# Banded attention and a top-1 mixture of experts: heads in row halves, loads reordered, one jump per expert

## The chip, the cores and the metric

The kernel runs on one core of one Trainium2 chip. The metric is the device time of one execution in microseconds. It was run three times: 770.36, 775.02 and 781.09 us, median 775.02. One further execution was taken with the hardware profiler; all rows of a profile below come from it.

The engines go by short names: PE is the matrix engine, with PEld for its loads of the stationary operand; DVE, ACT and POOL are the vector, scalar and general engine; SP issues most transfers. The transfers of all queues run on 16 DMA engines. PSUM holds PE's products; 512 columns of fp32 on 128 partitions are called a bank.

## What is computed

First a banded attention over 8 batches, 8 heads, 576 positions and 64 dimensions. Four heads look at the last 32 positions, four at every fourth of the last 128. Then the output, as 4608 tokens of 512 numbers, goes through a mixture of 8 experts, one expert a token.

```python
scores = scale * np.matmul(q, k.transpose(0, 1, 3, 2))
mask_plain = (rel >= 0) & (rel < window)                       # window 32
mask_dil = (rel >= 0) & (rel < window * dilation) & (rel % dilation == 0)
attn = softmax(np.where(masks, scores, -1e9))
x = np.matmul(attn, v) -> (4608, 512)
e_idx = np.argmax(x @ w_gate, axis=1)
for e in range(8):                                             # w1: 512 x 1024, w2: 1024 x 512
    h = np.maximum(x[mask] @ w1[e], 0.0)
    out[mask] = gate_w * sigmoid(x @ w_output_gate)[:, e] * (h @ w2[e])
```

## The kernel before

**Attention.** The host reorders the dilated heads by position modulo 4, so that all heads have the same band: a block of 32 queries needs its own block of 32 keys and the one before. The batches go in four pairs, each in nine steps (`NSTEP`); a step `g` holds four query blocks, on four strips of 32 partitions, for all 8 heads. Heads lie in pairs `hp`, two on 128 partitions (64 dimensions each).

Before the change the keys `kb` and the values `vb`, `v2` of a head pair stand as a block diagonal: head `c` fills 64 partitions, the other 64 are zero (`clear`). So one product of 128 rows does both heads:

```python
nc.tensor.matmul(sp[32*a : 32*a+32, P*hp : P*hp+P], lhsT=qb[b % 2][:, hp, 32*i : 32*i+32], rhs=keys, ...)
```

A step has 16 such products for the scores (L313) and 16 for the values (L370), each of 128 columns; in fp32 each shows as two passes in the profile. The step also has the mask, added by a product with the identity (L305), the maximum, subtraction and exponential (L326, L330, L336), the sums of a head on POOL (L341, L345, L347), the transposition of the probabilities (L358, copied by ACT at L360), the division (L384, L392), and the transposition of x for the routing (L426, copied at L432 and L435). The values are kept twice, `vb` and, shifted by 32 positions, `v2`; of `v2` half the lanes are loaded and half are copied from `vb` by DVE and ACT (`shift_v`, L290).

The loads of Q, K and V (`load_qk`, L273 and L276, and `load_v`, L282 and L285) are issued on SP, in between the stores of x to a scratch `xs` in DRAM (L402, L407). There are two sets of buffers, for the two batches of a pair; the loads of the next pair go out as soon as a batch is done. x has four buffers.

**Routing.** For each pair of batches, nine tokens to a partition: products with the gate weights, their transposition, the choice of an expert (`route_pick`), the rank within the expert (`rank_products`, `route_rank`), one-hot placements (`route_pay`, `route_spots`), and products that place the token numbers (`place_idx`, `place_scale`). The steps at which these parts run are written in two tables, `calm` and, for the third pair, `brisk`. Everything in the kernel keeps the order in which it is written (`manual_schedule`).

**Experts.** A token tile has 128 tokens; expert 0 starts with three tiles of the first three pairs (`head`) while the routing of the last pair runs beside it (`during_first`, `during_second`). The other experts take four tiles each (`BASE`), with up to two more where there are more tokens. Weights and activations are split into two parts of lower precision (`split_w`, L128 on ACT and L132 mostly on DVE), and each product is three (L204 for the first matrix, L835 for the second). Rows are gathered by POOL from `xs` (`gather4`, L162, four transfers a tile), turned by DVE and cast by ACT (`prep4`, L184, L191), and the results are scattered by POOL (L848). While an expert runs its second matrix, the weights and rows of the next are prepared; its first block of products (`start`) is issued at the end of the expert before. What depends on the number of tokens is reached by nested tests (`rest`, L1190), from the rarest case to the common one:

```python
with tc.If(flag[e] > bound) as more:
    body()
with more.Else():
    rest(less)
```

## Time and profile before

| | |
|---|---|
| three runs | 770.36, 775.02, 781.09 us |
| span of the profiled execution | 711.3 us |
| mean granted clock of PE | 0.940 |
| busy in the span | PE 597.4, PEld 476.4, DVE 351.5, ACT 261.1, POOL 372.3 us |
| transfers | 96.76 MB, mean 136 GB/s |

The span reaches from the first to the last instruction. The profiled execution's own time is not recorded beside it; the median of the runs is 63.7 us longer than the span, which is what lies around it. A row of grouped instructions names the line, engine, operation, `out<-in` and the count, then the busy time and the mean of one in ns, then the idle time ahead and what ended it. A row of waits names who waited for whom, the total in us, how often, and the longest. A row of a timeline begins with the start and the length in us. A row of a stretch gives its length, the busy time of PE, PEld, DVE, ACT and POOL, the granted clock, the share of the DMA engines, and GB/s.

### The profile page before, as it was taken

Reading aid. Unit: us, or ns where it says so; the run is one execution under the profiler, and the core shown is the slowest. Engines: PE = TensorE matmul, PEld = TensorE weight load, DVE = VectorE, ACT = ScalarE, POOL = GpSimd, SP = SyncE. Lnnn points to the kernel's source line nnn. Section 1 sums busy time; section 2 is a strip of 40 time slices with the busy share of each in tenths; the row PEclk is TensorE's granted clock in tenths of the full one; section 3 lists DMA queues with packets and bytes.
Section 4 is the critical chain, followed back from the end, with each engine's and each line's share of the span. In section 5 each row is a group of like instructions: output and inputs, shape, how many; then the busy total and the mean of one; then the engine's idle time right before and its main releaser. Section 6 shows DMA issues by size and latency. Waiting matters only on the chain. (4 is left out here: it accounts for less than half of the span.)

```text
span 711.3 us, 13438 instructions
## 1 busy us (share of the span) xinstructions
PE 597.4 (84%) x5077; PEld 476.4 (67%) x5109; DVE 351.5 (49%) x620; ACT 261.1 (37%) x449; POOL 372.3 (52%) x497
## 2 busy tenths in 40 slices
PE   5685877877677799998599999499999959989992
PEld 4464655655456789786488788388778748858891
DVE  5453476594796574364175164256237417526020
ACT  4464555545563322343153243143234214324010
POOL 7753446474474376476475177277247647525110
PEclk8998998998899799999799999899999979999997
DMA  8999899889945342154155144244205415511010
GB/s 203 217 257 213 195 237 242 220 198 228 265 109 178 98 146 77 50 158 146 44 162 159 37 141 134 99 135 144 89 23 173 138 47 159 157 45 30 16 46 30
DMA packets 55784, 96.76 MB, mean 136 GB/s; under 512 B 10107, under 2 KB 40317, under 8 KB 55680
## 3 DMA queue, kind: packets, MB, share of 16 engines
q1 hardware_dynamic: 46800, 76.44, 40.8%
q0 software_dynamic: 8880, 18.91, 8.3%
q8 instruction: 68, 1.11, 0.7%
q14 instruction: 36, 0.29, 0.2%
HBM read 79.57 MB, written 19.27 MB: 139 GB/s over the span
## 5 line engine op out<-in xcount | busy, mean ns | idle before, releaser
L162 POOL DMA_INDIRECT sd<-xs,idx x112 | 130.4, 1164 | 34.0 <-issue 31.8
L204 PE MATMUL ph<-sc,w 128*128 128x512 f32 x480 | 115.8, 399 | 20.6 <-issue 17.4
L204 PEld LDWEIGHTS ph<-sc,w 128*128 128x128 f32 x480 | 91.6, 193 | 43.9 <-issue 20.6
L848 POOL DMA_INDIRECT out_dram<-yt,idx x39 | 38.6, 990 | 98.9 <-ACT yt L844 52.7
L162 POOL DMA_INDIRECT xg<-xs,idx x56 | 60.8, 1086 | 47.6 <-PE ph L204 22.6
L341 POOL TENSOR_TENSOR half<-pt 128x256 f32<-128x256 f32 x34 | 26.1, 767 | 67.4 <-ACT pt L336 67.0
L835 PE MATMUL y<-w,h 128*128 128x512 f32 x190 | 53.7, 390 | 0.0
L210 ACT ACTIVATE h<-ph 128x512 fp32r<-128x512 f32 (+1 forms) x48 | 28.1, 586 | 67.1 <-PE ph L204 62.1
L211 DVE SCALAR_TENSOR_TENSOR h<-ph,h 128x512 fp32r<-128x512 f32 (+1 forms) x48 | 32.3, 675 | 37.0 <-ACT h L210 36.9
L345 POOL TENSOR_TENSOR half<-half 128x128 f32<-128x128 f32 (+3 forms) x136 | 43.2, 318 | 10.7
L132 DVE TENSOR_TENSOR w<-wraw,w 128x1024 fp32r<-128x1024 f32 x36 | 44.0, 1227 | 8.1 <-ACT w L128 8.1
L392 DVE TENSOR_TENSOR x<-av,rs 128x512 f32<-128x512 f32 x36 | 24.8, 688 | 45.1 <-DMA xs<-x 23.8
L191 ACT CAST sc<-sd 128x512 fp32r<-128x512 f32 x28 | 17.4, 620 | 75.6 <-DVE sd L184 60.5
L204 PE MATMUL ph<-sc,sa 128*128 128x512 f32 (+1 forms) x132 | 35.8, 408 | 9.3 <-issue 8.2
L835 PE MATMUL z<-w,h 128*128 128x512 f32 x152 | 43.5, 389 | 0.0
L128 ACT CAST w<-wraw 128x1024 fp32r<-128x1024 f32 x40 | 41.6, 1044 | 0.0
L835 PEld LDWEIGHTS y<-w,h 128*128 128x128 f32 x190 | 35.5, 188 | 7.3
L370 PE MATMUL av<-sc,pT 128*32 128x128 f32 x288 | 26.7, 312 | 15.5 <-ACT pT L360 7.2
L426 PE MATMUL tp<-idn,x 128*128 128x128 f32 x144 | 24.3, 293 | 17.3 <-DVE x L392 15.0
L204 PEld LDWEIGHTS ph<-sc,sa 128*128 128x128 f32 x132 | 26.1, 205 | 14.4 <-issue 8.7
L326 DVE TENSOR_REDUCE mx<-sp 128x8 f32<-128x512 f32 x36 | 23.8, 662 | 21.6 <-PE sp L313 21.6
L426 PEld LDWEIGHTS tp<-idn,x 128*128 128x128 f32 x144 | 15.8, 145 | 27.9 <-DVE x L392 14.3
(284 smaller groups left out, 1344.5 us busy)
## 6 DMA issues: line engine op xcount, KB each, us to landing
wraw<-in_w_dram SPq DMA_DIRECT2D x64, 512.0 KB, 4.3
xs<-x SPq DMA_DIRECT2D x40, 128.0 KB, 5.8
vb<-in_vv_dram SPq DMA_DIRECT2D x8, 448.0 KB, 6.4
qb<-in_qT_dram SPq DMA_DIRECT2D x3, 896.0 KB, 9.8
kb<-in_kT_dram SPq DMA_DIRECT2D x6, 448.0 KB, 10.6
sb<-in_vv_dram SPq DMA_DIRECT2D x8, 320.0 KB, 5.0
sd<-in_qT_dram SPq DMA_DIRECT2D x4, 512.0 KB, 7.8
sa<-in_kT_dram SPq DMA_DIRECT2D x8, 256.0 KB, 6.9
```

The costliest lines, as they stand in the source:

```text
L128: nc.scalar.copy(out=W[e, kind][0][c], in_=raws[e, kind, c])
L132: sub.tensor_tensor(out=w[1][c], in0=raws.pop((e, kind, c)), in1=w[0][c], op=ALU.subtract)
L162: nc.gpsimd.indirect_dma_start(out=xg[j][:, P * a : P * a + P], out_offset=None, in_=xs4, in_offset=bass.IndirectOffsetOnAxis(ap=idx4[:, a ...
L204: nc.tensor.matmul(ph[:, 0:m], lhsT=part_of(w, a, o, P), rhs=x[:, c, 0:m], start=k == 0, stop=k == 3 * NC - 1)
L210: nc.scalar.activation(out=hh, in_=ph[:, 0:m], func=AF.Relu)
L211: nc.vector.scalar_tensor_tensor(out=hl, in0=ph[:, 0:m], scalar=0.0, in1=hh, op0=ALU.max, op1=ALU.subtract)
L341: nc.gpsimd.tensor_tensor(out=half, in0=pv[:, :, 0:32], in1=pv[:, :, 32:64], op=ALU.add)
L345: nc.gpsimd.tensor_tensor(out=dst, in0=half[:, :, 0:n], in1=half[:, :, n : 2 * n], op=ALU.add)
L370: nc.tensor.matmul(av[32 * a : 32 * a + 32, P * hp : P * hp + P], lhsT=pT[:, hp, 32 * a : 32 * a + 32], rhs=src[:, :, hp, i // 2, :], star ...
L426: nc.tensor.transpose(out=tp[:, c], in_=x[:, P * c : P * c + P], identity=idn)
L835: nc.tensor.matmul(y, lhsT=l[:, r], rhs=part_of(w, a, DM * fc, DM), start=fc == 0 and n == 0, stop=fc == NF - 1 and n == 2)
L848: put = nc.gpsimd.indirect_dma_start(out=out, out_offset=bass.IndirectOffsetOnAxis(ap=at.bitcast(U32), axis=0), in_=yt, in_offset=None, bo ...
```

## The change

**Attention.** Keys and values stand without zero blocks: head `c` of a pair has its own 64 partitions in all of Q, K and V, which are loaded with 128 partitions. Scores and values become 32 products each of 64 rows and 64 columns (`scores`, `values`): two heads in the two row halves and four query blocks in the four column strips. Their results lie in two PSUM tiles of two banks (`sa`), one bank for each half, scores in the first 256 columns and values in the last. For the first two pairs the shifted V is copied whole by DVE and ACT (`first_shift`), for the last two half of it is loaded as before; for the last pair ACT copies the other half. x lies in halves of the stage buffers until step 26, and is copied for the routing in one piece (the order by classes moves into the read of `gate_products`). The first loads go out in the order of need, K and the first masks on ACT's queue.

**Order in a step.** The exponential moves into the next step; the transposition of x comes four steps behind its scores (three from step 27 on). PE's instructions of one step of the third pair, before, from the transposition of the probabilities to the first products of the values:

```order
L358 MATMUL tp<-idn,pt 128x128 [waits PE_49]
L358 MATMUL tp<-idn,pt 128x128 x3
L305 LDWEIGHTS cb
L305 MATMUL sp<-mk,cb 128x512
L313 MATMUL sp<-kb_108,qb_109 32x128 x16
L426 MATMUL tp<-idn,x 128x128 [waits DVE_49,Activation_49]
L426 MATMUL tp<-idn,x 128x128 x3
L370 MATMUL av<-v_111,pT 32x128 [waits DVE_49,Activation_49]
L370 MATMUL av<-vb_110,pT 32x128 [waits DMAHW3_49,DMAHW1_49]
```

And after, from the scores of one step to the values of the next:

```order
L330 MATMUL s_95<-sa_104,sd_106 32x64 x32
L379 MATMUL tp<-idn,pt 128x128 [waits DVE_49,Activation_49]
L379 MATMUL tp<-idn,pt 128x128 x3
L317 LDWEIGHTS cb
L317 MATMUL s_94<-mk,cb 128x256 [waits DVE_49]
L317 LDWEIGHTS cb
L317 MATMUL s_94<-mk,cb 128x256
L453 MATMUL tp<-idn,wraw 128x128 [waits Activation_49]
L453 MATMUL tp<-idn,wraw 128x128 x3
L393 MATMUL s_95<-sc_110,pT 32x64 [waits DVE_49,Activation_49]
L393 MATMUL s_95<-sb_108,pT 32x64
```

The products on the full array (transpositions, mask) now stand together, and so do those in strips: the scores stand behind the values of an earlier step instead of between the transpositions.

**Routing.** The parts run at other steps, most of them later, and over more steps for the first two pairs. The nine comparisons of `route_spots` become one, the counts are taken along with the ranks. In the first expert the ranks of the last pair come one block of products later, and its four subtractions of weights go from POOL to DVE.

**Experts.** The number of the case is computed on the chip (`path`), read at the middle of an expert (`choose`), together with a hint for the jump, and one `Switch` replaces the nested tests; the check for rare repairs behind expert 0 is such a jump too. PE at the end of the first expert that has the tests, before:

```order
L835 MATMUL z<-sb,h_3436 128x512
L204 MATMUL ph<-sc,w_3414 128x512 [waits Activation_49]
L204 MATMUL ph<-sc,w_3414 128x512 [waits DVE_49]
L204 MATMUL ph<-sc,w_3414 128x512 x10
L1182 TENSOR_LOAD cnt
L1190 COMPARE_AND_BRANCH
L204 MATMUL ph<-sc,w_3414 128x512 x12
L204 MATMUL tpx<-xxh,w_3415 128x256 [waits PE_49]
```

And after:

```order
L881 MATMUL z<-sb,h_4398 128x512
L206 MATMUL ph<-sc,w_4376 128x512 [waits Activation_49]
L206 MATMUL ph<-sc,w_4376 128x512 [waits DVE_49]
L206 MATMUL ph<-sc,w_4376 128x512 x10
L1430 SWITCH_STRIDE
L1430 ISA x2
L1267 BRANCH_PREFETCH_HINT
L206 MATMUL ph<-sc,w_4376 128x512 x12
L1430 UNCONDITIONAL_BRANCH
```

The load of the count has gone to the middle of the expert; behind the jump stands, in each of the five bodies, a hint for its own end. The gathers of rows change their order: of expert `e+1` the tiles 2 and 3 go ahead of the rare tiles of `e`, and tiles 0 and 1 of `e+2` are gathered at the end of `e`. The rare tiles are turned during the second matrix instead of at the end of the first, and every second pair of blocks of the first matrix takes PSUM banks of another pool.

```diff
-        ps_s = actx.enter_context(tc.tile_pool(name="ps_s", bufs=2, space=PSUM))
-        ps_a = actx.enter_context(tc.tile_pool(name="ps_a", bufs=2, space=PSUM))
+        ps_s = actx.enter_context(tc.tile_pool(name="ps_s", bufs=1, space=PSUM))
+        sa = [ps_s.tile([P, 2, 512], F32, name=f"s{i}") for i in range(2)]
...
+        def load_q(b, j0, j1):
+            s = slice(64 * j0, 64 * j1)
+            nc.sync.dma_start(out=qb[b % 2][:, :, s], in_=qT[b, :, :, s])
+
+        def load_k(eng, b, j0, j1):
+            eng.dma_start(out=kb[b % 2][:, j0:j1], in_=kT[b, :, j0:j1])
...
+        def load_vv(b):
+            load_v(b, 0, 9)
             for c in range(2):
+                r = lanes(c, 1)
+                nc.sync.dma_start(out=v2[b % 2][r, :, 1:9], in_=vv[b, r, :, 0:8])
...
+        def mask(g):
+            m = mk[:, subs_of(g)[0]].rearrange("p (h c k) -> p h c k", h=4, c=2)
+            for c in range(2):
+                nc.tensor.matmul(
+                    sa[g % 2][:, c, 0:256].rearrange("p (h k) -> p h k", h=4), lhsT=idb, rhs=m[:, :, c],
+                    start=True, stop=False, skip_group_check=True,
+                )
...
         def scores(g):
-            var, subs = subs_of(g)
-            sp = ps_s.tile([P, 512], F32, name="sp")
-            nc.tensor.matmul(sp, lhsT=idb, rhs=mk[:, var], start=True, stop=False, skip_group_check=True)
+            _, subs = subs_of(g)
             for hp in range(4):
-                for a, (b, i) in enumerate(subs):
-                    je = i // 2
-                    jo = (i - 1) // 2 if i else 0
-                    keys = _free(
-                        kb[b % 2], je * 256 + hp * 32, [[2304, 2], [128 + (jo - je) * 256, 2], [1, 32]]
-                    )
-                    nc.tensor.matmul(
-                        sp[32 * a : 32 * a + 32, P * hp : P * hp + P],
-                        lhsT=qb[b % 2][:, hp, 32 * i : 32 * i + 32],
-                        rhs=keys,
...
-                    )
-            st[g, "s"] = sp
+                for c in range(2):
+                    r = slice(64 * c, 64 * c + 64)
+                    for a, (b, i) in enumerate(subs):
+                        je = i // 2
+                        jo = (i - 1) // 2 if i else 0
+                        nc.tensor.matmul(
+                            sa[g % 2][32 * a : 32 * a + 32, c, 64 * hp : 64 * hp + 64],
+                            lhsT=qb[b % 2][r, hp, 32 * i : 32 * i + 32],
+                            rhs=_free(kb[b % 2][r], je * 256 + hp * 32, [[128 + (jo - je) * 256, 2], [1, 32]]),
...
+                        )
...
         def values(g):
             _, subs = subs_of(g)
             pT = st.pop((g, "p"))
-            av = ps_a.tile([P, DM], F32, name="av")
             for hp in range(4):
-                for a, (b, i) in enumerate(subs):
-                    src = vb[b % 2] if i % 2 else v2[b % 2]
-                    nc.tensor.matmul(
-                        av[32 * a : 32 * a + 32, P * hp : P * hp + P],
-                        lhsT=pT[:, hp, 32 * a : 32 * a + 32],
-                        rhs=src[:, :, hp, i // 2, :],
...
-                    )
-            st[g, "av"] = av
+                for c in range(2):
+                    r = slice(64 * c, 64 * c + 64)
+                    for a, (b, i) in enumerate(subs):
+                        src = vb[b % 2] if i % 2 else v2[b % 2]
+                        o = 256 + 64 * hp
+                        nc.tensor.matmul(
+                            sa[(g + 1) % 2][32 * a : 32 * a + 32, c, o : o + 64],
+                            lhsT=pT[r, hp, 32 * a : 32 * a + 32],
+                            rhs=src[r, hp, i // 2, :],
...
+                        )
...
-            x = wk.tile([P, DM], F32, name="x", bufs=4)
+            if g >= 26:
+                x = wk.tile([P, DM], F32, name="x", bufs=4)
+            else:
+                if g % 2 == 0:
+                    st["rows"] = stage.tile([P, 1024], F32, name="wraw")
+                x = st["rows"][:, DM * (g % 2) : DM * (g % 2) + DM]
...
-                nc.scalar.copy(out=xT[:, 0:2, o + s0 : o + s0 + n], in_=tp[:, 0:2, p0 : p0 + n])
-                for c, i0, q0, m in class_pieces(s0, n):
-                    f0 = o + NCLS * i0 + c
-                    nc.scalar.copy(
-                        out=xT[:, 2:4, f0 : f0 + NCLS * (m - 1) + 1 : NCLS], in_=tp[:, 2:4, p0 + q0 : p0 + q0 + m]
-                    )
...
+                nc.scalar.copy(out=xT[:, :, o : o + n], in_=tp[:, :, p0 : p0 + n])
...
         def route_spots(pr):
             ohp = R["ohp"] = rt.tile([P, NSTEP, P], BF16, name="ohp")
-            for c in range(NSTEP):
-                nc.vector.tensor_scalar(
-                    out=ohp[:, c], in0=iot, scalar1=R["pos"][:, c : c + 1], scalar2=None, op0=ALU.is_equal
-                )
+            TP = [P, NSTEP, P]
+            nc.vector.tensor_tensor(
+                out=ohp, in0=bc(iot.unsqueeze(1), TP), in1=bc(R["pos"].unsqueeze(2), TP), op=ALU.is_equal
+            )
...
-        clear(nc.vector, kb[0], 0)
...
-        clear(nc.vector, vb[1], 0)
+        for t in v2:
+            nc.gpsimd.memset(t[:, :, 0], 0.0)
...
-        nc.sync.dma_start(out=cb, in_=cbf)
-        nc.sync.dma_start(out=mk[:, 0:1], in_=cmask[:, 0:1])
-        load_qk(0, 0, 2)
+        nc.sync.dma_start(out=idb, in_=cbf[:, 0:P])
+        load_q(0, 0, 2)
...
+        nc.scalar.dma_start(out=mk[:, 0:1], in_=cmask[:, 0:1])
+        load_k(nc.scalar, 0, 0, 2)
+        nc.scalar.activation(out=warm, in_=zero, func=AF.Exp)
+        nc.scalar.dma_start(out=mk[:, 1:2], in_=cmask[:, 1:2])
+        load_k(nc.scalar, 0, 2, 4)
+        load_k(nc.scalar, 0, 4, 9)
...
-            4: dict(late=[rank_products], post=[route_rank]),
+            3: dict(late=[rank_products, route_rank]),
...
         for g in range(last + 1):
             if g >= 2:
                 transpose_p(g - 2)
-                inverse(g - 2)
+            if g < last:
+                mask(g)
+            if g >= 1:
+                softmax(g - 1)
+            if 4 <= g <= hurry:
+                transpose_x(g - 4)
+            if g >= hurry:
+                transpose_x(g - 3)
...
             if g >= 2:
                 values(g - 2)
-            routing(g, "ahead")
+                inverse(g - 2)
+                output(g - 2)
+                load(g - 2, load_vv if g > NSTEP + 2 else whole_v)
             if g < last:
-                softmax(g)
-            if g >= 2:
-                output(g - 2)
-                load(g - 2, load_v)
-            if g in (last - 3, last - 1):
-                late_sum(g)
-            shift(0, g)
+                scores(g)
+                shifted(g)
...
             if 33 <= g < 36:
-                split_lo(0, 0, g - 33, nc.gpsimd)
+                split_lo(0, 0, g - 33, nc.vector)
...
+    def choose(e):
+        flag[e] = nc.values_load(cnt[0:1, 2 * E + 3 + e : 2 * E + 4 + e], min_val=0, max_val=len(PATHS))
+        flag[e, "hint"] = tc.switch_hint({t: flag[e] for t in ENGINES}, len(PATHS) + 1, f"paths{e}")
...
-        elif k == 1:
+        elif k == 2:
             rank_products(pr)
             route_rank(pr)
             load_w(1, 0)
-        elif k == 2:
+        elif k == 3:
             route_pay(pr, nc.vector)
             route_rows(pr)
             route_spots(pr)
-        elif k == 4:
+        elif k == 5:
             place_idx(pr)
             finish_idx(perm, pm, idx, E * SLOTS, rt)
-            nc.vector.tensor_copy(out=st[pr, "lt"][1][:, 0 : E * SLOTS], in_=idx)
+            nc.vector.tensor_copy(out=st[pr, "lt"][:, 512 : 512 + E * SLOTS], in_=idx)
             for j in range(HEAD, HEAD + 2):
                 gather(j, where(0, j)[0])
-        elif k == 5:
             scale_exp(pr)
             scale_pick(pr)
             scale_gate(pr)
-        if k < 4:
-            split_w(0, 1, k, nc.gpsimd)
+        if 0 < k < 5:
+            split_w(0, 1, k - 1)
...
+    for n in tc.Switch(flag["rare"], 2, flag["rare", "hint"]):
+        products1(1, 1, *X, BASE * P, ph, (1, 2, 3))
+        if n:
+            repair()
...
-            h.append(base_h(e, fc, X, BASE * P))
+            h.append(base_h(e, fc, X, BASE * P, ph=bank(ps_x, "tpx") if fc % 4 > 1 else None))
             if fc == 2:
-                gather4(e, 4)
-                gather4(e, 5)
-                next_gathers(e + 1)
+                rows_of(e + 1, *((2, 3) if e > 1 else range(BASE)))
+                rows_of(e, 4, 5)
             if fc < 6:
                 split_w(e, 1, fc - 2)
                 if fc == 5 and e + 1 < E:
                     load_w(e + 1, 0)
-            if fc >= 6:
-                prep4(fc - 2, *xx, fc - 6)
+        choose(e)
         ys = [bank(ps_y, "y"), bank(ps_z, "z"), bank(ps_y, "y"), bank(ps_z, "z")]
         for fc in range(NF):
             for j in range(BASE):
@@ -1174,23 +1238,16 @@
                 if fc == 3:
                     load_w(e + 1, 1)
                 prep4(fc, *X, fc)
+            if fc in (4, 5):
+                prep4(fc, *xx, fc - 4)
+            if fc == 5:
+                rows_of(e + 2, 0, 1)
...
-        def rest(paths):
-            (bound, body), *less = paths
-            if not less:
-                body()
-                return
-            with tc.If(flag[e] > bound) as more:
-                body()
-            with more.Else():
-                rest(less)
...
+        bodies = [
+            nothing,
+            lambda: extra(e, BASE, xx, 0, 1, fill),
+            lambda: extra(e, BASE, xx, 1, 0, fill),
+            lambda: extra(e, BASE, xx, 1, 1, fill),
+            two,
+        ]
+        for n in tc.Switch(flag[e], len(bodies), flag[e, "hint"]):
+            bodies[n]()
```

355 lines of the change are left out of this document (186 added, 169 removed).

## The prediction

> **What bounds the kernel now.** I read the slices of the page first, then stretches of my own choosing, then the waits, the transfers, and last the instructions of single steps. In the slices each digit is the busy share of a fortieth of the span (17.8 us).
>
> ```profile
> PE   5685877877677799998599999499999959989992
> DMA  8999899889945342154155144244205415511010
> GB/s 203 217 257 213 195 237 242 220 198 228 265 109 178 98 146 77 50 158 146 44 162 159 37 141 134 99 135 144 89 23 173 138 47 159 157 45 30 16 46 30
> ```
>
> For eleven slices the DMA engines are full at 200 to 260 GB/s while PE is at 5 to 8 tenths; afterwards it is the other way round, with PE at 9 and single dents. The same by stage, with the exponentials (one a step) that set the borders:
>
> ```profile
> L336 ACT ACTIVATE pt<-pt x36: 612/631/664, 9.7 to 203.9; 128x512 f32<-128x512 f32 x36
> 9.70:203.90 194.20, 141.68 (x2681) 106.09 (x2712) 115.06 (x272) 97.35 (x205) 105.19 (x255) 0.90 0.95 224
> 203.90:292.00 88.10, 77.95 (x541) 67.13 (x542) 53.64 (x120) 29.60 (x56) 48.71 (x42) 0.94 0.34 112
> 292.00:697.10 405.10, 371.78 (x1779) 297.99 (x1777) 175.39 (x223) 126.06 (x183) 208.48 (x187) 0.97 0.33 102
> ```
>
> Columns of a stretch: length, busy PE, PEld, DVE, ACT, POOL, granted clock, DMA share, GB/s. The 36 attention steps take 194.2/35 = 5.55 us each; PE is busy 141.7 of 194.2, DVE 115.1, ACT 97.4, POOL 105.2, and only the DMA engines (0.95) are full. Who waits there says the same (first 200 us):
>
> ```profile
> DVE x L392 <- DMA xs<-x: 23.8, 9, 5.6
> ACT sc L290 <- DMA sb<-in_vv_dram: 21.1, 5, 7.6
> ACT v L290 <- DMA vb<-in_vv_dram: 18.4, 6, 5.1
> PE sp L313 <- DMA sa<-in_kT_dram: 6.3, 2, 5.6
> ```
>
> V arrives late at the copies, K late at PE, and the rows of x leave late, so that their four buffers are not free. Attention is bound by transfers. From 292 us on PE is the bound, with 405.1 - 371.8 = 33.3 us idle; between the two lies the first expert with 88.1 - 78.0 = 10.1 us idle.
>
> **The transfers.** Bytes do not explain the 224 GB/s; the shape does. Alone on the engines were part of a Q load on 128 partitions (71.1 to 71.65 us), of a K load on 64 (73 to 76) and of the V loads on 64 and 32 (133.5 to 136.8):
>
> ```profile
> 71.10:71.65 0.55, 0.55 (x20) 0.50 (x13) 0.00 (x0) 0.55 (x1) 0.46 (x2) 0.50 1.05 381
> 73.00:76.00 3.00, 2.86 (x48) 1.72 (x41) 1.08 (x2) 2.11 (x5) 0.04 (x1) 1.00 0.96 186
> 133.50:136.80 3.30, 3.15 (x65) 2.42 (x61) 2.17 (x6) 1.45 (x3) 2.01 (x5) 1.00 1.08 209
> ```
>
> The last number is GB/s: 381 against 186 and 209. The change loads K and V with 128 partitions. Q, K and V are 9.44 MB each (8*576*512*4 bytes). At 381 GB/s the three take 74 us; rows of x, 9.44 MB, at 300 (my choice between 224 and 381, for 1 KB pieces) 31 us; the shifted V that is still loaded (four of eight batches, half the lanes, 2.1 MB) at 209 GB/s 10 us; weights and constants some 8 us. Together 123 us where 194 were full. So transfers stop being the bound if the step is longer than 123/36 = 3.4 us.
>
> **What a step costs then.** In one step of before, undisturbed by transfers, PE shows:
>
> ```profile
> 101.50 1.33 PE L313 MATMUL sp<-sa,sd 128*32 128x128 f32 x32
> 105.05 0.66 PE L358 MATMUL tp<-idn,pt 128*128 128x128 f32 x4
> 105.85 0.81 PEld L313 LDWEIGHTS sp<-sa,sd 128*32 128x32 f32 x32 [0.32 <-issue]
> 105.85 1.08 PE L313 MATMUL sp<-sa,sd 128*32 128x128 f32 x32
> 106.90 0.65 PE L426 MATMUL tp<-idn,x 128*128 128x128 f32 x4
> 248.58 0.55 PE L939 MATMUL tp<-lt,idn 128*32 128x48 f32 x32
> ```
>
> The 16 products of the scores are 32 passes, four column strips side by side, in 1.08 us; the values have the same shape. After the change there are twice as many, of 64 columns and 64 rows, eight side by side. No row of before has 64-row halves, so I bound them. Upper end: the halves do not overlap, and 64 passes of half the columns cost the same 1.08 us. Lower end: they overlap fully, half, 0.54. L939 gives 32 passes of 48 columns, four abreast, in 0.55 us with the tail of the last (0.21); that is 0.34 us of starts, 10.7 ns each, so 64 starts need at most 0.69 us. I take 0.66 a group, nearest to that row: a gain of 0.42, twice a step. The order within a step also changes: both transposes and the mask first, then values and scores, so that PE changes between the full array and strips twice instead of four times; one such change is the 0.32 us of "issue" above. PE's step: 0.66 + 0.65 + 0.2 (mask, estimated) + 2*0.66 + 2*0.32 = 3.5, less what the tails overlap, say 3.3 us.
>
> DVE, ACT and POOL keep nearly all of their work. DVE's share:
>
> ```profile
> L392 DVE TENSOR_TENSOR x<-av,rs 128x512 f32<-128x512 f32 x17 | 11.7, 687 | 26.6 <-DMA xs<-x 16.6 <-PE av L370 10.0
> L330 DVE TENSOR_TENSOR pt<-sp,mx 128x512 f32<-128x512 f32 x16 | 11.1, 692 | 1.5
> L326 DVE TENSOR_REDUCE mx<-sp 128x8 f32<-128x512 f32 x16 | 10.5, 658 | 6.9 <-PE sp L313 6.9
> L384 DVE RECIPROCAL rs<-sm 128x8 f32<-128x8 f32 x16 | 3.0, 188 | 0.0
> L567 DVE TENSOR_SCALAR ohp<-cb,pos x36: 234/244/2439, 117.7 to 239.0; 128x128 bf16<-128x128 bf16 x36
> L132 POOL TENSOR_TENSOR w<-wraw,w x4: 2331/2353/2370, 223.5 to 239.0; 128x1024 fp32r<-128x1024 f32 x4
> L132 DVE TENSOR_TENSOR w<-wraw,w x36: 1214/1225/1268, 255.0 to 612.7; 128x1024 fp32r<-128x1024 f32 x36
> ```
>
> Four a step make 0.69 + 0.69 + 0.66 + 0.19 = 2.2 us, 80 of the 115 busy us. The other 35 are shifts of V and routing. Nine spot comparisons (9*0.244) become one of the same elements, perhaps 1.2 us: minus 3 for three pairs. Three subtractions of weights come from POOL: plus 3*1.225 = 3.7. So DVE stays near 116 us, of which 36, or 1.0 a step, are uneven. If they lie on five steps of nine, those take 2.2 + 0.3 for the hand-overs (estimated) + 1.8 = 4.3 us, and the other four PE's 3.3: (5*4.3 + 4*3.3)/9 = 3.9. Between this and 4.35, the distance from one scores group to the next in the step of before (105.85 - 101.50), I take 4.0, nearer to the first. The routing that moves to a later step keeps its instructions on DVE, POOL and PE, and the first gathers still go out three steps before the end; the same sum holds it. ACT gets one copy a step for x transposed in place of two to five: it has 97 us of work before, less after, and is no bound. The eight half-tile memsets go; POOL's and ACT's are hidden today behind the first transfers, and DVE's too; the first exponential, at 9.7, comes perhaps 1 us sooner since the first K and mask go out on ACT's queue. K on ACT's queue costs ACT five issues at the start, while it has nothing else. Q, K and V of a batch become one transfer each where there were two or three, on SP: fewer issues, no new wait. Rows of x pass to eight half buffers until step 26, so that a late landing holds up nobody.
>
> Steps of 4.0 in place of 5.55: 35*1.55 = 54 us, plus 1 at the start: **55**. Ends: PE's 3.3 (80 us) and the 4.35 (43 us).
>
> **The first expert.** Three waits of PE belong to routing:
>
> ```profile
> PE tp L504 <- DVE oh L495: 4.0, 1, 4.0
> PE perm L573 <- DVE ohp L567: 3.4, 2, 2.1
> ```
>
> One block of products more stands between the choice and the ranks, and the placing comes a block later: the 4.0 goes, the 3.4 goes in part. Against that, DVE takes four subtractions from POOL, 4*1.225 = 4.9 us, in the same stretch; they are late next, ahead of the placing. The load of the second expert's weights goes out a block later too, and is read some eight blocks after that. Between 0 and 7.4 I take **5**.
>
> **The other experts.**
>
> ```profile
> L1190 PEldq COMPARE_BRANCH  x26: 70/340/4714, 334.6 to 692.7; - x26
> 334.09 2.81 PE L204 MATMUL ph<-sc,w 128*128 128x512 f32 x11 [0.22 <-DVE sc L192]
> 346.06 4.31 PE L204 MATMUL ph<-sc,w 128*128 128x512 f32 x11 [9.16 <-issue]
> PE ph L204 <- issue: 25.6, 3, 9.2
> PE ph L204 <- ACT sc L191: 3.2, 3, 1.3
> PE y L1053 <- DMA out_dram<-yt,idx: 1.9, 1, 1.9
> PE y L1043 <- ACT sa L210: 1.6, 1, 1.6
> ```
>
> Where an expert has no more than four tiles, PE walks through nested tests, three of them taken at over 3 us each (the maximum is 4.7), and stands still for 8.2 to 9.2 us; three experts do so, 25.6 us. Afterwards eleven products take 4.31 us instead of 2.81, at the reduced clock: 3*1.5 = 4.5 us more. The change has one jump by an index that was read a half expert earlier, with a hint to fetch the target. What a hinted jump costs no row shows. Lower end 0.07 us (the minimum above, no fetch); upper end 3.5 for the jump and 3.5 for leaving the body. Cover: the queue holds the twelve products of the next expert's first block, 2.8 us, and the body that most take holds twelve more. I take 0.6 for each of seven: 25.6 + 4.5 - 4.2 = 26. The rows of the next expert are gathered two tiles earlier, ahead of the rare tiles; the 3.2 us of waits for the cast go, less what the later rare tiles cost, 2. The gathers are the same in number, POOL is busy 208 of 405 us there, so they stay hidden. Together **28**.
>
> The Trainium skill (Runtime: NRT & Kernel Launch, Instruction fetch mechanics) says prefetch is sequential and a taken jump outside the window must fetch before it goes on; the rows above agree at over 3 us. It knows no hint, and by it alone the jump would still fetch: that is the second rival's result.
>
> **The sum.** The page's span is 711.3 us; the median of three runs is 775.0, so 63.7 us lie around the span (59 to 70 over the runs 770.4 to 781.1), and I keep 63.7. 711.3 - 55 - 5 - 28 = 623; 623 + 64 = **687 us**.
>
> **Rivals.**
> 1. Transfers stay the bound. If 128-partition K and V run at the mean of today, 224 GB/s, then 42 MB take 188 us; attention gains only 6, the time is 775 - 6 - 5 - 28 = 736. For it: the 381 was seen in short stretches. Against: every Q load shows it. Chance 0.08.
> 2. Hints do not help: 7 us of fetch for each of seven, less 2.8 + 1.5 of cover, leaves 2.7*7 = 19 us where I had 4: 687 + 15 = 702. Chance 0.15.
> 3. PE becomes the bound by its starts:
>
> ```profile
> 97.08 0.37 PE L511 MATMUL tp<-oh,ones 128*128 128x8 bf16 x9
> ```
>
> Eight columns wide, nine products still need 0.37 us, (0.37 - 0.17)/8 = 25 ns from start to start. If the 128 passes of a step had that floor, they would take 3.2 us in place of 1.3: the step is 3.3 + 1.9 = 5.2 us, attention gains 13, and the time is 729. L939's 10.7 ns speaks against it, with strips of columns but not of rows. Chance 0.07. The Trainium skill (TensorEngine Tiling (Array Packing), Instruction Overhead) says this: some 60 cycles for each product, and no tiling of a dimension that is already small; by it halving 128 columns to 64 gains nothing. L939 disagrees.
> 4. Slower than before: each change of the 64-row half drains PE as the change of strips does, 0.32 us. The loop changes halves eight times in a group, 16 a step: 5.1 us more, steps of 8.4, attention 35*2.85 = 100 us longer, time 775 + 100 - 33 = 842. It decides from (54 + 34)/35 = 2.5 us a step, 0.16 us for each change of half. No row speaks for it, since strips change without gaps. Chance 0.04.
>
> **How the numbers follow.** My forecast has 0.62, with 656 (3.3 us a step, 7 and 32 elsewhere) to 705 (4.35 and less from the jumps); rivals as above; 0.04 is left for no change, some stall that I do not see. The likeliest is 687. The range goes from 656 to 740, which takes in rivals 1 to 3. Within 2% is about what a measurement of this kernel can tell from no change: 759.5 to 790.5. Faster 0.62 + 0.15 + 0.08 + 0.07 = 0.92, same 0.04, slower 0.04.
>
> **What would show it.** DMA share in the attention stage under 0.9 at 250 GB/s or more; exponentials from under 9 to about 149 us; scores of 64 passes in about 0.7 us; DVE busy over 75% of that stage; no wait of x for its own transfer; no "issue" gap over 2 us between experts; PE idle in the first expert about 5 us. Wrong if PE's groups take over 1.1 us, if loads stay near 200 GB/s, or if PE's queue shows seven fetches over 3 us.

## The result, and the profile after

| | before | after |
|---|---|---|
| runs, median | 772.69 us (765.35 to 781.09) | 736.78 us (731.88 to 738.95) |
| ratio | | 0.9605, 95% interval 0.9541 to 0.9668 |
| span, and the same execution's own time | 711.3 us, not recorded | 736.6 us, 738.36 us |
| granted clock, whole span | 0.940 | 0.897 |

The kernel is faster by 36 us, where 88 were forecast. The span after is longer than the span before, and only 1.8 us lie around it: the page of before shows an execution some 60 us quicker than the runs beside it.

The slices of the page after (a digit is the busy share of a fortieth of the span, 18.4 us; PEclk is the granted clock in tenths):

```profile
PE   5656747767578994897899999899999899899991
PEclk8767877798798998899799999799999899999996
DMA  9744475486623362024336314334505234320010
GB/s 308 267 145 172 128 251 170 138 271 212 201 74 116 132 188 94 15 82 148 107 113 191 120 47 144 116 117 131 164 23 155 79 129 145 115 69 26 30 39 22
```

The transfers are no longer full, as forecast; but PE is no fuller, and its clock is lower. The exponentials that set the borders of the attention, and the two stretches (length, busy PE, PEld, DVE, ACT, POOL, clock, DMA share, GB/s):

```profile
L357 ACT ACTIVATE pt<-pt x36: 631/632/637, 8.9 to 226.9; 128x512 f32<-128x512 f32 x36
8.87:226.85 217.98, 145.11 (x4907) 111.18 (x4906) 121.18 (x268) 103.51 (x180) 99.92 (x253) 0.78 0.59 191
226.85:720.72 493.87, 457.47 (x2369) 366.31 (x2367) 223.70 (x342) 154.57 (x233) 239.88 (x219) 0.96 0.34 104
```

A step takes 217.98/35 = 6.23 us, not 4.0, and more than the 5.55 of before. No engine and no transfer is full in this stage (PE 145 of 218, DMA share 0.59). Who waits there, from the waits of after in the attention (us in sum, times, longest):

```profile
PE s L330 <- issue: 34.8, 13, 6.5
PE s L393 <- issue: 20.2, 11, 3.9
PE tp L453 <- issue: 3.6, 1, 3.6
PE tp L379 <- issue: 2.1, 1, 2.1
PE s L393 <- DVE pt L347: 2.8, 4, 0.8
```

The same answer for the attention of before has hardly any such wait:

```profile
PE tp L426 <- DVE x L392: 12.9, 9, 2.7
PE sp L313 <- issue: 1.3, 4, 0.4
```

"issue" means that the profile shows nothing that the engine waits for: 34.8 + 20.2 + 3.6 + 2.1 = 60.7 us, or 1.7 a step, and PE stands in the middle of a group whose operands are all there. One such place in the timeline of after (start, length, what, idle before):

```profile
59.28 0.48 PE L330 MATMUL s<-sa,sd 64*32 64x64 f32 x29
59.51 0.69 DVE L419 TENSOR_TENSOR wraw<-s,rs 128x512 f32<-128x512 f32 x1 [0.74 <-PE s L393]
61.35 0.23 POOL L370 TENSOR_SCALAR sm<-sm 128x8 f32<-128x8 f32 x1
65.17 0.50 PEld L330 LDWEIGHTS s<-sa,sd 64*32 64x32 f32 x34 [5.58 <-issue]
65.17 0.74 PE L330 MATMUL s<-sa,sd 64*32 64x64 f32 x34 [5.41 <-issue]
```

After 29 of 64 passes PE stops for 5.4 us, DVE and POOL run out of work, and then the group goes on. What arrives in such waits is on a queue of its own that the page calls instruction (16 KB packets; packets, MB, share):

```profile
q8 instruction: 80, 1.31, 0.8%
```

(The page has a second queue of that name, with packets of 8 KB; it brings 8 of them in the attention, where this one brings some 40.) Its packets, set beside PE's waits of over 1 us (seven of the 18, times in us, worked out from the records of the packets; the DMA share is that of the 2 us ahead of the block):

```
PE stops  goes on   wait   block from  lasts  after the block before  DMA share in the 2 us ahead
 39.88     42.06    2.18     39.44     1.14          4.08                  0.96
 46.23     49.81    3.58     47.35     0.96          7.91                  0.93
 54.30     55.59    1.29     53.24     0.93          5.88                  0.00
 59.75     65.17    5.41     62.58     1.10          9.35                  1.00
105.08    109.96    4.89    107.35     1.30          9.17                  1.05
179.02    180.82    1.80    178.48     0.94          4.00                  0.94
184.65    191.11    6.46    188.50     1.09         10.02                  0.81
```

All 18 waits end 1.24 to 1.60 us after a block has landed. Counted in the records, PE starts 255 to 257 products and weight loads from one of these waits to the next, or two, three, four or six times as many: it stops where 256 instructions end, and 256 is then what a block holds. Blocks are never closer than 3.2 us; where the DMA engines were under half busy between two blocks the mean distance is 4.2 us (20 of them), where they were busier 6.9 (19). Some 276 recorded PE instructions a step (2 x 4966/36, from the fullest records) are more than one block of 256 a step; in before it was 2 x 2712/36 = 151. This is the first theory, and a theory only so far: PE outruns the supply of its instructions, and bulk loads delay that supply.

A wait also costs the clock. The same place in stretches of 2 us:

```profile
60.00:62.00 2.00, 0.00 (x0) 0.00 (x0) 0.20 (x1) 0.46 (x1) 1.22 (x5) 1.00 1.05 406
62.00:64.00 2.00, 0.00 (x0) 0.00 (x0) 0.00 (x0) 0.00 (x0) 0.00 (x0) 0.56 0.96 350
64.00:66.00 2.00, 0.83 (x39) 0.66 (x43) 0.00 (x0) 0.00 (x0) 0.00 (x0) 0.50 0.42 150
66.00:68.00 2.00, 2.00 (x14) 1.01 (x14) 1.84 (x3) 0.40 (x1) 0.00 (x0) 0.50 0.05 11
68.00:70.00 2.00, 2.00 (x80) 1.74 (x81) 0.75 (x2) 1.69 (x3) 0.39 (x1) 0.73 0.00 0
70.00:72.00 2.00, 2.00 (x87) 0.95 (x72) 1.73 (x3) 1.32 (x4) 1.61 (x6) 1.00 0.17 51
```

The clock (third number from the right) halves some 2.5 us into the wait, which begins at 59.75, and is back at 1.00 only about 4 us after PE goes on. The Trainium skill (TensorE: Matmul & The Clock Gate, What's actually happening) states half rate after an idle window of about 3.4 us and full rate after as long a busy one; the return after 4 us agrees, while the drop after 2.5 us of waiting comes sooner than a whole idle window.

### The profile page after: what moved, and what is told of

Its sections match the earlier page's. It is cut to its first block, busy times and chain, and to the rows that moved or that the text cites. A ratio compares the mean times of both kernels' runs of the same rounds, so it can differ in the third digit from the quotient of the medians.

```text
span 736.6 us, 18376 instructions
## 1 busy us (share of the span) xinstructions
PE 608.9 (83%) x7448; PEld 483.1 (66%) x7449; DVE 346.3 (47%) x614; ACT 260.3 (35%) x416; POOL 341.7 (46%) x482
## 5 line engine op out<-in xcount | busy, mean ns | idle before, releaser
L330 PE MATMUL s<-sa,sd 64*32 64x64 f32 x2304 | 40.3, 253 | 36.2 <-issue 34.8
L206 PE MATMUL ph<-sc,w 128*128 128x512 f32 x240 | 57.6, 391 | 0.0
L330 PEld LDWEIGHTS s<-sa,sd 64*32 64x32 f32 x2304 | 31.8, 117 | 39.2 <-issue 38.5
L206 PE MATMUL tpx<-sc,w 128*128 128x512 f32 x240 | 56.2, 390 | 0.8 <-DVE yt L1138 0.8
L206 PEld LDWEIGHTS tpx<-sc,w 128*128 128x128 f32 x240 | 44.9, 188 | 10.8 <-PE ph L206 1.2
L206 PEld LDWEIGHTS ph<-sc,w 128*128 128x128 f32 x240 | 44.7, 188 | 10.7 <-issue 1.7
L393 PE MATMUL s<-sb,pT 64*32 64x64 f32 x1152 | 37.0, 246 | 13.4 <-issue 13.3
L393 PE MATMUL s<-sc,pT 64*32 64x64 f32 x1152 | 36.3, 245 | 12.4 <-issue 6.9
L345 DVE TENSOR_REDUCE mx<-s 128x8 f32<-128x512 f32 x36 | 24.8, 690 | 44.2 <-PE s L330 44.1
L393 PEld LDWEIGHTS s<-sc,pT 64*32 64x32 f32 x1152 | 27.7, 117 | 23.1 <-issue 14.9
```

Source lines behind the costliest of these rows:

```text
L206: nc.tensor.matmul(ph[:, 0:m], lhsT=part_of(w, a, o, P), rhs=x[:, c, 0:m], start=k == 0, stop=k == 3 * NC - 1)
L330: nc.tensor.matmul(sa[g % 2][32 * a : 32 * a + 32, c, 64 * hp : 64 * hp + 64], lhsT=qb[b % 2][r, hp, 32 * i : 32 * i + 32], rhs=_free(kb[b ...
L345: nc.vector.tensor_reduce(out=mx, in_=sp, axis=AX.X, op=ALU.max)
L393: nc.tensor.matmul(sa[(g + 1) % 2][32 * a : 32 * a + 32, c, o : o + 64], lhsT=pT[r, hp, 32 * a : 32 * a + 32], rhs=src[r, hp, i // 2, :], ...
```

## The experiments

The time of one and the same kernel differs from chip to chip: before took 773 us on the first chip, 746 to 753 on the second, 716 on the third and 714 on the fourth. So kernels are compared within a chip, and the attention by its step, which differs little.

### Is the span of before what its runs take? (second chip)

The kernel before, unchanged.

> The kernel before, once more, for its profile beside its own time. The page of before had a span of 711.3 us, while its timed executions took 765 to 781; the page of after had a span of 736.6 beside a time of 738.4. Theory A (the profiled execution of before was a quick one, nothing lies around the span): span and time agree here to 2 us, at 760 to 780, with the attention steps longer than the 5.55 us that the page of before showed, 6.5 to 7.5. Theory B (some 60 us do lie around the span of before): span 711 again and time 770.

Span 751.0 beside a time of 752.8: nothing but 1.8 us lies around it, theory A is right in that and theory B falls. A's steps are wrong, though: they take 5.47 us as before. The time lies in the experts:

```profile
9.79:201.41 191.62, 145.79 (x2712) 106.06 (x2712) 115.47 (x272) 97.12 (x204) 104.97 (x254) 0.91 0.94 227
201.41:736.81 535.40, 468.44 (x2318) 375.41 (x2318) 228.37 (x342) 155.12 (x239) 256.93 (x229) 0.93 0.31 95
```

535 us where the page of before had 493, at a lower clock. The attention of before changes little between these two executions (191.6 and 194.2 us); what differs is the experts' stage.

### After on the same chip, and the order of the two halves

> The kernel after, as a base for the runs beside it on the same chip: 737 us, attention 6.2 us a step, PE waiting for 'issue' in the middle of scores and values some 55 us in sum over 36 steps.

```profile
8.75:226.06 217.31, 145.18 (x4966) 111.46 (x4967) 121.17 (x268) 103.28 (x181) 100.43 (x253) 0.80 0.60 192
```

745.93 us, and 6.21 us a step with 63 us of "issue" waits (35.5 + 19.6 + 3.7 + 2.4 + 1.8). On this chip before was at 746.11 with a spread of 731 to 766; beside its two quickest runs, 731 and 735, after takes 2% longer. Neither a gain nor a loss can be told there. The next kernel puts the loop over the halves outside, in `scores` and in `values`:

```diff
-            for hp in range(4):
-                for c in range(2):
+            for c in range(2):
+                for hp in range(4):
```

> After, with the loop over the two row halves outside the loop over head pairs in scores and values: the half changes once in a group instead of seven times, the number of instructions is the same. Theory 1 (PE waits for its instructions, which come in blocks of 16 KB not less than 4 us apart): attention stays at 6.2 us a step, the time within 1% of after. Rival 2 (a change of the half drains PE, 0.16 us each): 12 changes fewer a step, about 1.9 us a step, 60 to 70 us less, about 670.

6.23 us a step, with 47.3 us of "issue" waits, 750.94 us (740 to 763). A change of the row half costs nothing that can be seen; rival 2, which is rival 4 of the prediction, falls.

### Fewer, and more, PE instructions

Half of the value products of after left out:

```diff
-                for c in range(2):
+                for c in range(2 if g < 2 else 1):
                     r = slice(64 * c, 64 * c + 64)
```

> After, with half of the value products left out from step 2 on (head 1 of each pair keeps old numbers), so 64 instructions of some 290 a step fewer on PE; no other engine has less to do. Theory 1 (instruction supply): PE's blocks in attention fall from 41 to about 32, and the step falls by 0.8 to 1.6 us, 30 to 55 us less than after, about 690. Rival 3 (PE's own time: the left-out products are busy for some 0.35 us of a step): at most 0.4 us a step, 14 us. Rival 4 (DVE, ACT or transfers set the step): no change.

```profile
9.81:193.84 184.03, 135.51 (x3879) 103.89 (x3880) 121.48 (x268) 102.57 (x180) 103.01 (x253) 0.81 0.68 225
```

184.03/35 = 5.26 us a step, 0.95 less than beside it, and 34.6 us of "issue" waits; 32 blocks land instead of 40. Rival 3 allowed 0.4 us and rival 4 nothing, so both fall. The time as a whole (1020 us) says nothing, since the wrong values send the tokens to other experts. The reverse, on the kernel before: the same products cut in two, all else as it was.

```diff
+                    for c in range(2):
+                        o = P * hp + 64 * c
...
-                        sp[32 * a : 32 * a + 32, P * hp : P * hp + P],
+                            sp[32 * a : 32 * a + 32, o : o + 64],
...
-                        rhs=src[:, :, hp, i // 2, :],
+                            rhs=src[:, c, hp, i // 2, :],
...
```

> The kernel before, with each product of scores and values cut into two of 64 columns (one for each head, still 128 rows with the zero block): the same result, 64 PE instructions more in each of the products' two groups' passes, as many as the kernel after has. Nothing else changes. Theory 1 (PE waits for its instructions): some 36 blocks of 16 KB in the attention stage where before had 22, PE waiting for 'issue' inside the groups 30 us or more in sum, and steps of 6.0 to 6.6 us where before had 5.5. Rival 5 (it is the 64-row halves, or the new order of the step, that cost): steps stay at 5.5, hardly any 'issue' wait.

```profile
9.71:225.55 215.84, 160.94 (x4918) 123.43 (x4919) 114.96 (x272) 99.14 (x204) 107.05 (x257) 0.91 0.83 202
PE sp L312 <- issue: 22.5, 13, 3.6
PE av L371 <- issue: 21.1, 12, 4.1
```

6.17 us a step where before has 5.47, with 48.6 us of "issue" waits (two smaller rows bring 5.0), and 39 blocks where before has 22. The 18 waits of over 1 us again lie 256 recorded instructions apart, or a multiple of it, to within one. The old products, loads and order become as slow as the new ones by the number of instructions alone. Theory 1 is shown by this pair; rival 5 falls. It is a single execution, though the waits inside it can be counted.

### What the loads do to the instruction blocks

In after only the first pair is loaded, and computed again for the others:

```diff
-        loads = {4: 0, 8: 1}
+        loads = {}
```

> After, without the loads of Q, K and V for the pairs 2 to 4, which are computed again from the data of the first pair; PE, DVE, ACT and POOL have the same instructions in attention. Theory 1a (a block of instructions needs 4 us, whatever else runs): the blocks stay as they are, 'issue' waits of some 55 us, steps of 6.2. Theory 1b (bulk loads delay the blocks: in after and its repetition the spacing is 7 to 10 us where the DMA share in the gap is near 1, and 4 us where it is not): no spacing over 7 us after the first pair, 'issue' waits fall to 10 to 25 us and the steps to 5.0 to 5.4. The time as a whole depends on the changed routing and says nothing.

```profile
8.39:187.76 179.37, 138.64 (x4914) 106.63 (x4903) 121.03 (x268) 102.77 (x181) 102.03 (x253) 0.83 0.33 103
PE s L330 <- issue: 21.4, 14, 2.7
PE s L393 <- issue: 5.2, 6, 2.3
```

5.13 us a step, as 1b has it, and 27.2 us of "issue" waits, 2.2 above its range. Blocks come 3.4 to 7.9 us apart, 4.5 in the mean; one is over the 7 us that 1b allowed. So some 36 of the 63 us of waits that after has on this chip come from the loads, and the rest remains without them. Where in the transfer engines a block is held up is not visible. As a remedy, the loads in three pieces each:

```diff
...
-        loads = {4: 0, 8: 1}
+        loads = {4: (0, 0, 3), 5: (0, 3, 6), 6: (0, 6, 9), 8: (1, 6, 9), 9: (1, 0, 3), 10: (1, 3, 6)}
...
```

> After, with the loads of a batch's Q, K and V for the later pairs in three pieces each, issued over seven steps instead of at two. Theory 1b: shorter bursts, so the blocks are late less often: attention at 5.6 to 6.0 us a step instead of 6.2, time 8 to 20 us less than after. Theory 1a: 6.2, as after. Rival: pieces of 768 bytes make the transfers slower and the steps longer, over 6.3.

5.96 us a step (208.59/35), within the range of 1b; 746.05 us beside 753.16 for before, ratio 0.9861 (0.9806 to 0.9916). The steps gain 9 us in the profiled execution, but the time is that of after on this chip: the 8 to 20 us that were expected are not seen in it. The profiled execution was among the longer of the ten, at 751.08 us, with 515.8 us in the experts' stage against 498.8; it can't say where the 9 us went.

### The halves of the change apart

The kernel before with the experts of after (`choose`, `Switch`, `rows_of`, the first expert's order), nothing of the attention. Its core:

```diff
-            next_gathers(e + 1)
+            rows_of(e + 1, *((2, 3) if e > 1 else range(BASE)))
...
-        rest([
...
+        for n in tc.Switch(flag[e], len(bodies), flag[e, "hint"]):
+            bodies[n]()
```

> The kernel before up to the first expert, with the experts of after (one jump with a hint, rows ahead, the first expert's routing a block later). Attention 192 to 194 us as before (5.5 us a step). If the experts' part of the change is what gained: from the last exponential to PE's end 470 to 495 us where before had 493 in its quick execution and 535 in the other, no 'issue' gap over 4 us behind the jumps, and a time of 700 to 720, below both kernels. If the jump gained nothing: 735 to 770 as before.

723.9 us (712.7 to 732.1; 700 to 720 was expected) where before had 753.2: the experts' part alone gains more than the whole. It was run again on two other chips, and on the fourth beside after:

> The kernel of e8 unchanged, as the base of e9 and e10 on the same chip: 713 to 732 us again, 20 to 40 under before.

665.69 us, ratio 0.9306 (0.9273 to 0.9338): 50 us under the 715.66 of before there, more than expected.

> The kernel after on the same chip as the two beside it, since the kernel before took 773, 746 to 753 and 716 us on the chips so far. If e8's part (the experts) gains and the attention loses: after stands 18 to 26 us above the kernel of e8 on this chip, that is 688 or so on a chip where before takes 716, and the attention is 217 us against 191 to 199.

> The kernel of e8 (attention of before, experts of after) as the third point on this chip: 30 to 50 us under before, 18 to 26 under after.

On the fourth chip: before 714.20, after 685.72 (ratio 0.9614, 0.9569 to 0.9659), the old attention with the new experts 666.47 (0.9325, 0.9287 to 0.9363). So the experts' part is worth 47.7 us and the attention's part costs 19.3 (in the two profiled executions the attention stages differ by 15.5; the old attention took 190.9 to 199.3 us in four profiles of the mixed kernel, so this size is good to a few us). Their stages, first after, then the mixed kernel:

```profile
9.11:221.93 212.82, 145.51 (x4966) 112.30 (x4967) 121.20 (x268) 103.28 (x180) 99.99 (x253) 0.78 0.61 196
221.93:665.94 444.01, 437.30 (x2372) 356.88 (x2370) 223.90 (x342) 154.44 (x233) 245.13 (x219) 1.00 0.37 116
```

```profile
9.91:207.28 197.37, 150.75 (x2712) 109.09 (x2712) 115.39 (x272) 97.06 (x204) 104.93 (x254) 0.88 0.94 220
207.28:652.83 445.55, 439.29 (x2318) 358.73 (x2318) 226.62 (x351) 156.24 (x239) 251.86 (x225) 1.00 0.37 116
```

The experts take 444 and 446 us at full clock. In the page of before, whose span fits this chip's runs, they took 493.2 us with 43.5 idle (88.1 + 405.1, PE 78.0 + 371.8); here 6.7 us are idle and 12.4 us less are busy. This sets a page of the first chip beside one of the fourth, where before was timed, but not profiled with all its loads. The longest waits of PE left in after's experts on this chip:

```profile
PE tpx L206 <- DVEq L1267: 1.2, 1, 1.2
PE y L881 <- issue: 1.1, 1, 1.1
```

### The hint, and a second queue for the loads (third chip)

Two variations of the mixed kernel. Without hints:

```diff
-        flag[e, "hint"] = tc.switch_hint({t: flag[e] for t in ENGINES}, len(PATHS) + 1, f"paths{e}")
...
-        for n in tc.Switch(flag[e], len(bodies), flag[e, "hint"]):
+        for n in tc.Switch(flag[e], len(bodies)):
```

> The kernel of e8 without the hints: the jump through the table stays, nothing says ahead where it goes. If the hint makes the jump cheap (the branches of PE at the bodies' entries took 0.3 to 0.4 us with it): PE's branch now takes over 3 us at each of the seven experts, as in the tests of before, PE idles some 3 to 5 us behind four or more of them, time 8 to 25 us over e8's. If the hint does nothing and the single jump is what gained: the same as e8 within 1%.

664.95 us, beside 665.69 with hints: no difference. The branches of PE (minimum, median, maximum in ns), without hints and with:

```profile
L1384 PEldq COMPARE_BRANCH  x16: 300/2402/4228, 272.9 to 640.4; - x16
```

```profile
L1386 PEldq COMPARE_BRANCH  x16: 293/320/4186, 282.9 to 651.9; - x16
```

The hint does shorten them, from a median of 2.4 to 0.3 us, though five of the 16 still take over 3 us with it, where eight do without. The products queued ahead cover the 3 to 4 us all the same: beside the eight PE idles once for 1.3 us and once for 0.2. In before each of the three waits of 8.2 to 9.2 us lies over three such branches in a row. So of the jump's part, one jump in place of a chain is what gained; the other pieces of the experts' part, as the order of the gathers, were not run apart. Then the second head's loads on ACT's queue:

```diff
-                nc.sync.dma_start(out=kb[z][r, c, j0:j1], in_=kT[b, r, j0:j1])
+                eng = nc.scalar if c and b > 1 else nc.sync
+                eng.dma_start(out=kb[z][r, c, j0:j1], in_=kT[b, r, j0:j1])
...
```

> The kernel of e8 (attention of before, experts of after), with the loads for the second head of each pair (K, V and the shifted V on partitions 64 to 127, batches 2 to 7) issued on ACT's queue beside those for the first head on SP's, so that both halves of the partitions are written at the same time. Transfers were at 186 to 209 GB/s in stretches with 64 partitions, at 381 with 128. Theory 6 (the shape is the limit, and with two queues both halves run together): DMA at 260 GB/s or more in the attention stage, steps of 4.6 to 5.2 us instead of 5.5 to 5.7, time 15 to 35 us under e8's. Rival 7 (queues share what there is, or ACT's own work is held up behind its issues): steps of 5.5 to 5.9, no gain.

669.75 us (0.9391, 0.9347 to 0.9434), 5.62 us a step, 221 GB/s at a DMA share of 0.91: no gain. Here two queues on two halves of the partitions are no substitute for one transfer on 128.

### The step without each of its two obstacles

After, with the upper halves of the numbers only:

```diff
+        def top(a):
+            return a.bitcast(BF16)[..., 1::2]
...
-                            lhsT=qb[b % 2][r, hp, 32 * i : 32 * i + 32],
+                            lhsT=top(qb[b % 2][r, hp, 32 * i : 32 * i + 32]),
...
```

> After, with the products of scores and values reading only the upper 16 bits of each number (as bf16): one pass each instead of two, so 128 PE instructions a step fewer and the same number of products in 64-row halves; the results are coarser, the routing may differ in a few tokens. Theory 1 with 1b (instructions): blocks in attention fall from 41 to about 23, 'issue' waits from 57 us to under 15, steps to 4.2 to 5.0 us, which is near the 4.0 of the forecast. If the step then stays over 5.5, something else that the forecast did not see (the row halves, the order of the step, the DVE's work) holds it.

```profile
8.62:158.21 149.59, 106.93 (x2759) 75.95 (x2760) 119.33 (x268) 102.40 (x181) 102.24 (x249) 0.83 0.84 275
PE s L317 <- DVE wraw L422: 16.3, 12, 4.1
PE s L333 <- issue: 4.1, 2, 3.4
```

149.59/35 = 4.27 us a step, 4.9 us of "issue" waits (0.8 in a smaller row), 22 blocks, 620.92 us (0.8689 of before, 0.8641 to 0.8737). Row halves, order and loads are those of after. PE now waits for DVE, which is busy for 80% of the stage. (A single pass also takes less PE time, so not all of the 1.8 us a step is supply; and the results are coarser, so this is no replacement for after.) And the kernel before, without the later loads:

```diff
-        loads = {4: [(0, 0, 5)], 5: [(0, 5, 9)], 8: [(1, 7, 9), (1, 0, 7)]}
+        loads = {}
```

> The kernel before without the loads of Q, K and V for the pairs 2 to 4, computed again from the first pair's data. If transfers bound the attention of before, as the prediction said: steps fall from 5.5 to 4.2 to 4.6 us (scores group to scores group took 4.35 in a step that transfers did not hold up). If its engines or its order bound it: 5.2 or more. The time as a whole depends on the changed routing.

```profile
9.71:167.12 157.41, 136.42 (x2712) 99.16 (x2712) 115.54 (x272) 98.31 (x204) 107.79 (x257) 0.96 0.49 122
```

157.41/35 = 4.50 us a step: transfers did bound the attention of before. All attention stages together (instructions are recorded products and weight loads of PE a step; waits are PE's for "issue"):

| kernel | instructions | loads | waits, us | step, us |
|---|---|---|---|---|
| before (page; second chip) | 151 | yes | 1.3; 0.9 | 5.55; 5.47 |
| before, no later loads | 151 | no | 0 | 4.50 |
| before, products cut in two | 273 | yes | 48.6 | 6.17 |
| after (page; second chip; fourth) | 273 to 276 | yes | 60.7; 63.0; 53.7 | 6.23; 6.21; 6.08 |
| after, loop over halves outside | 273 | yes | 47.3 | 6.23 |
| after, loads in pieces | 276 | yes | 52.5 | 5.96 |
| after, half the values | 216 | yes | 34.6 | 5.26 |
| after, no later loads | 273 | no | 27.2 | 5.13 |
| after, one pass | 153 | yes | 4.9 | 4.27 |

## Why the prediction was wrong

**The step that failed is the attention's step of 4.0 us, the term of 55.** It was built from the durations of products and the work of DVE; how many instructions PE has to be supplied with was never counted, though the change doubles the products and each shows as two passes with a weight load of its own. In its place the runs show 6.1 to 6.2 us: instead of 35 x 1.55 us gained, 23.8 us lost between the two pages (217.98 against 194.16) and 19.3 between two kernels on the fourth chip. The number of instructions alone does it (the cut products on the old attention), and the loads make it worse (without them the waits more than halve).

Two parts of that step were right. That transfers bound the attention is shown by the run without them (4.50; the step quoted from before gave 4.35), and that 128-partition loads would free them too: 0.59 x 218 = 129 us of full engines, where 123 were forecast. The first exponential came 0.8 us sooner, of 1 forecast. With the supply out of the way the step is 4.27, inside the bounds of 3.3 to 4.35, but with one pass for each product; that 4.0 could be had with two is not shown. The group of scores was sized too low, 62 passes in 0.82 us where 0.66 was taken, inside its bounds of 0.54 to 1.08.

**The 63.7 us around the span do not exist.** I took the difference of two executions for a fixed cost. An execution and its span differ by 1.7 to 1.9 us in every run since but one, which has 3.9. With 1.8, my sum would have been 711.3 - 88 + 1.8 = 625, so this mistake and the first one pull in opposite directions, and the result lies inside the range only for that reason. It is luck as well that after took 685.72 us on the fourth chip, so near to 687: before took 714.20 there, and the gain is 28, not 88. The page of before showed an undisturbed execution, and the first chip's runs took 60 us more. After's page from that chip has such disturbance as well: its experts take 494 us, the same kernel's on the fourth chip 444.

**The experts: mechanism right, size too small.** 5 + 28 = 33 forecast, 47.7 between kernels on the fourth chip. The idle time went from 43.5 to 6.7 us, 36.8, near the 25.6 of the jumps, the few of the waits and the 5 of the first expert together; the part that was sized too low is the busy time, 12.4 us less where I had 4.5 for the slow clock behind the jumps. In the page of before the stretches with the jumps stand at 0.90 to 0.93 of the clock, here at 1.00. That the rest of the 12.4 is the clock too was not tried.

**The rivals.** 1 (transfers stay) is refuted by the DMA share of 0.59. Its time, 736, is the measured one, and so nearly is rival 3's 729, but neither for its reason: 62 starts in 0.82 us are 13 ns or less each, not 25. (What I drew there from the 60 cycles of the Trainium skill (TensorEngine Tiling (Array Packing), Instruction Overhead), that halving 128 columns gains nothing, does not follow from them alone, since 64 columns are still more than 60.) In 2 the premise holds, since the time without hints is the same, but its price does not: the uncovered 2.7 us a jump do not appear, the queued products cover it. 4 is refuted by the outer loop. The rule of the Trainium skill that I quoted for the jump also has a sentence on supply (Runtime: NRT & Kernel Launch, Instruction fetch mechanics): crossing a 16 KiB block is "mostly hidden". This case disagrees, with 60.7 us of PE's waits in 218, at the ends of 256 instructions.

**What I left out** is in one row that I did not quote: the queue of instructions. It was in the page of before, with 68 packets. After's 40 blocks in the attention at 4 to 7 us each are longer than the 144 us that I forecast for the whole stage.

Still open: why the chips differ, and what holds a block up behind the loads.

## What to carry to other kernels

Count PE's instructions before cutting a product into smaller ones: each block of 256 took 4.2 us here and near 7 beside bulk loads. From these, an estimate: a stage that is denser than some 60 instructions a microsecond (256/4.2), or 37 beside bulk loads, has to wait, however short its products are. Take a change apart before keeping it: the two halves of this one are worth -48 and +19 us, and the first without the second is the fastest version found here that computes the whole reference (0.9325 of before, where the whole has 0.9614). Compare a span with the time of its own execution only.

## What the hardware showed unexpectedly

- Blocks of PE's instructions (16 KB) landed no closer than 3.2 us, and PE went on 1.2 to 1.6 us after they had landed.
- After a wait of 5.4 us the granted clock was 0.50 and came back to 1.00 about 4 us after PE went on, so by an estimate (4 us at half the clock) a wait costs up to 2 us more than its length.
- The same kernel's experts took 444 us on one chip and 494 on another. Part of it is one place, the two rare tiles of expert 0. On the first chip:

```profile
280.00:290.00 10.00, 3.03 (x19) 2.71 (x18) 0.85 (x2) 0.77 (x2) 7.65 (x8) 0.88 0.19 54
290.00:300.00 10.00, 5.08 (x24) 4.79 (x23) 0.85 (x2) 1.08 (x3) 3.36 (x4) 0.50 0.21 79
```

and on the fourth:

```profile
275.00:285.00 10.00, 10.00 (x80) 9.78 (x79) 3.26 (x8) 2.68 (x7) 7.62 (x8) 1.00 0.20 54
```

PE is idle for 11.9 us of 20 and at half clock in the one, full in the other. On the first chip ACT and DVE stand still there as well, twice for 7.4 to 7.5 us, for nothing that the profile names. The kernel before shows the same on the second chip, so it does not come from the change:

```profile
270.00:280.00 10.00, 3.19 (x15) 2.60 (x13) 0.42 (x1) 0.38 (x1) 6.80 (x7) 0.67 0.30 103
```
